# Soft-capped attention and two MLPs on one Trainium2 core: batches 2 and 3 begin twelve slots later

## The chip, the cores and the metric

The kernel runs on one core of a Trainium2 chip. Its engines are TensorE (PE, with its weight loads shown as PEld), VectorE (DVE), ScalarE (ACT), GpSimd (POOL) and SyncE (SP), which here only issues DMAs. The metric is the device time of one execution in microseconds. Each engine takes its instructions in the order in which the built program has them.

## The reference

```
attention, per batch b (4) and head h (12), 448 rows of 64:
  s = q k^T / 8 ; s = cap * tanh(s / cap) ; p = softmax(s) ; o = p v
x  = the heads of o side by side: 1792 rows (4 batches of 448) x 768
h  = max(x w_in, 0)                 768 -> 2048
x2 = h * h @ w_out                  2048 -> 768
h2 = x2 w_in2 ; g = h2 * sigmoid(1.702 h2)
out = g @ w_out2                    1792 x 768
```

All inputs are 32- or 64-bit floats: the weights come as 64-bit words and are put together on the chip.

## The kernel before

**Precision.** A float is split into a high part that TensorE multiplies in one pass and a low part (the rest). A product takes three matmuls of 448 columns: high by high, high by low, low by high.

**MLP units.** The work on one batch's 448 rows is a pass. A pass is 68 units (`PER`): per layer 16 of kind "a" (one block of 128 hidden columns, 18 matmuls, L1240, with an evaluation on ACT and DVE and a split into the tile `g`) and 18 of kind "b" (one block of 128 output columns over 5 or 6 hidden blocks, 15 or 18 matmuls, added into `y`). Below, u0 to u67 are the first pass, u68 to u135 the second, and so on. A unit's weights are split two units ahead, ACT writing `wh` (L1220) and DVE `wl` (L1221). In the first pass the 64-bit words are also loaded from the inputs (L1161), turned into floats (ACT `sx` L1196, DVE `y32` L1203) and stored to DRAM (`keep`, L1214); later passes load those (L1172).

**Attention slots.** A pair is two heads of one batch; there are 24, six to a batch. A pair's steps stand in a table of slots (`PLAN`, for batches 0 and 1 `PLAN0`). Loads of q, k are at slot -17; the preparation of `kk` and `qq` (DVE transposes L840, splits L893, L900, L918, L925, and for batches 2 and 3 a DMA on POOL's queue, L906, that copies half of `kk`) at -8 to -3; then four chunks, two slots apart, each of scores on TensorE (`sps`, L955), tanh and exp on ACT (L966, L970), for batches 2 and 3 a split of the exponentials (ACT `phi` L977, DVE `plo` L981), and the product with v on TensorE (`vps`, L1009). Taking the sums (L1056), the division (L1040, L1042) and so on follow up to slot 15 or 19. `sps` has two buffers, so the third chunk's scores wait for the first chunk's tanh.

**How the two meet.** Batch 0's attention stands before the first pass. During pass s (L1349 to L1361) the slots of batch s+1 are spread over the units, `begin` saying at which slot each pair starts: 8 slots to a pair, and 14 later (`LATE`) for batches 1 to 3, which leaves slots between batch 0's last work and batch 1's first. `ready(b)` is the last slot of batch b. Pairs of the batch behind fall into the slots up to `ready(s + 1)` as well, where their own slots lie below it.

**What sets the order.** The building layer lists all instructions in the order in which these loops emit them and then schedules them by its own estimate of readiness, so an instruction can end up units before or behind the place where it was emitted. What an engine meets is that schedule, shown below where the change moves it.

Names: `mps` is a unit's accumulator, `xt` the input of a pass, `x32` an attention output before its split, `vt` and `vs` tiles of v, `e` the exponentials, `vps` the product with v, `o` a transposed block of the result that POOL's queue stores (L1298).

Of the kernel before, what the change touches and what calls it, by code (L numbers as in the profile page):

```python
# [677 lines left out]
def bounded_cap(ctx, tc, q, k, v, cap, w1, w2, w3, w4, out):  # L678
# [46 lines left out]
    XZ = 2  # L725
    PA = 1
    PB = 4
    LATE = 14

    EARLY = (10, 11)  # L730
    LA = (5, 4, 3, 2)
# [60 lines left out]
    pairs = [(b, p) for b in range(B) for p in range(NP)]  # L792
# [314 lines left out]
        PLAN[2 * c + 4].append((add_keys, c))  # L1107
    ORDER = sorted(set(PLAN) | set(PLAN0), reverse=True)

    begin = [8 * n + (LATE if b else 0) for n, (b, p) in enumerate(pairs)]  # L1110
    first_slot = {t: n for n, t in enumerate(begin)}

    last_split = []
# [264 lines left out]
@with_exitstack  # L1378
def softcap_attention_mlp_mlp(ctx, tc, q, k, v, cap, w1, w2, w3, w4, out):

    nc = tc.nc
    pool = ctx.enter_context(tc.tile_pool(name="flag", bufs=1))
    c = pool.tile([1, 2], F32, name="capsize")
    over = pool.tile([1, 1], I32, name="over")
    nc.sync.dma_start(out=c[:, 0:1], in_=cap.rearrange("(o n) -> o n", o=1))
    nc.vector.tensor_scalar(c[:, 1:2], c[:, 0:1], -1.0, None, ALU.mult)
    nc.vector.tensor_tensor(c[:, 0:1], c[:, 0:1], c[:, 1:2], ALU.max)
    nc.vector.tensor_scalar(over, c[:, 0:1], CAP_MAX, None, ALU.is_gt)
    bounded_cap(tc, q, k, v, cap, w1, w2, w3, w4, out)
    flag = nc.values_load(over, min_val=0, max_val=1)  # L1390
    with tc.If(flag > 0):
        any_cap(tc, q, k, v, cap, w1, w2, w3, w4, out)
# [30 lines left out]
```

## Time and profile before

| | us |
|---|---|
| median of 3 runs | 1208.37 (1207.05 to 1210.19) |
| the profiled execution, device time | 1208.87 |
| its span, first to last instruction | 1207.1 |
| TensorE matmul busy | 1162.8 (96% of the span) |
| DVE busy | 820.2 (68%) |
| ACT busy | 748.2 (62%) |

In this execution the first product of the first pass starts at 79.4 us, u44 at 291.7, u72 at 437.2, the third pass (u136) at 692.4 and the fourth (u204) at 963.3. Times below count from the span's start. In rows of engine sums each pair is busy time with the number of instructions in brackets, and PEclk is TensorE's mean granted clock, 1.00 being 2.4 GHz.

### The profile page before, as it was taken

Reading aid. Unit: us, or ns where it says so; the run is one execution under the profiler, and the core shown is the slowest. Engines: PE = TensorE matmul, PEld = TensorE weight load, DVE = VectorE, ACT = ScalarE, POOL = GpSimd, SP = SyncE. Lnnn points to the kernel's source line nnn. Section 1 sums busy time; section 2 is a strip of 40 time slices with the busy share of each in tenths; the row PEclk is TensorE's granted clock in tenths of the full one; section 3 lists DMA queues with packets and bytes.
Section 4 is the critical chain, followed back from the end, with each engine's and each line's share of the span. In section 5 each row is a group of like instructions: output and inputs, shape, how many; then the busy total and the mean of one; then the engine's idle time right before and its main releaser. Section 6 shows DMA issues by size and latency. Waiting matters only on the chain.

```text
span 1207.1 us, 15331 instructions
## 1 busy us (share of the span) xinstructions
PE 1162.8 (96%) x5532; PEld 1005.7 (83%) x5532; DVE 820.2 (68%) x1135; ACT 748.2 (62%) x1105; POOL 70.0 (6%) x157
## 2 busy tenths in 40 slices
PE   7889999989889999999999999999999999999996
PEld 4459778768767889998898899989999999999995
DVE  3577376765778995789688885888665753565454
ACT  6889676766777774576776666677653444344431
POOL 1000000000000220000000320000000220000000
PEclk9999999989899999999999999999999999999999
DMA  4469778677867965535443643333222442333333
GB/s 110 109 195 295 222 224 254 213 227 214 251 196 223 281 181 136 147 92 140 114 123 103 159 131 104 94 107 105 89 82 97 143 134 92 116 107 110 106 99 49
DMA packets 196583, 180.32 MB, mean 149 GB/s; under 512 B 118290, under 2 KB 167442, under 8 KB 196498
## 3 DMA queue, kind: packets, MB, share of 16 engines
q1 hardware_dynamic: 186706, 168.14, 46.5%
q0 software_dynamic: 4224, 10.43, 3.8%
q10 hardware_dynamic: 5568, 0.69, 0.4%
q8 instruction: 46, 0.75, 0.3%
q14 instruction: 39, 0.32, 0.1%
HBM read 142.25 MB, written 30.67 MB: 143 GB/s over the span
## 4 chain that ended last, share of the span: by engine, by line
PE 92%; ACT 5%; DVE 1%; issue 1%; DMA 0%; SPq 0%; DVEq 0%; ACTq 0%
PE mps L1240 79%; PE vps L1009 7%; PE sps L955 5%; ACT e L970 1%; ACT e L966 1%; PE sums L1056 1%; ACT ct L1024 1%; ACT phi L977 0%; ACT wh L1220 0%; ACT qq L918 0%; ACT kk L893 0%; PE qps L844 0%; PE kps L844 0%; ACT sx L1196 0%; DMA qt<-in_q_dram 0%
## 5 line engine op out<-in xcount | busy, mean ns | idle before, releaser
L1240 PE MATMUL mps<-g,wh 128*128 128x448 f32 x1536 | 442.6, 369 | 4.8 <-ACT wh L1220 4.8
L1240 PE MATMUL mps<-xt,wh 128*128 128x448 f32 x1536 | 441.5, 369 | 4.4 <-DVE x L1026 2.7
L1220 ACT ACTIVATE wh<-wraw 128x768 fp32r<-128x768 f32 (+1 forms) x204 | 164.7, 808 | 261.8 <-PE mps L1240 248.1
L1240 PEld LDWEIGHTS mps<-g,wh 128*128 128x128 f32 x1536 | 289.0, 189 | 36.9 <-ACT wh L1220 5.9
L1240 PEld LDWEIGHTS mps<-xt,wh 128*128 128x128 f32 x1536 | 289.6, 189 | 34.4 <-DVE x L1026 3.4
L1240 PE MATMUL mps<-xt,wl 128*128 128x448 f32 x768 | 284.7, 371 | 0.0
L1240 PE MATMUL mps<-g,wl 128*128 128x448 f32 x768 | 282.9, 369 | 1.0 <-DVE wl L1221 1.0
L1221 DVE TENSOR_TENSOR wl<-wraw,wh 128x768 fp32r<-128x768 f32 (+1 forms) x204 | 185.2, 908 | 135.9 <-ACT wh L1220 132.9
L1240 PEld LDWEIGHTS mps<-g,wl 128*128 128x128 f32 x768 | 145.1, 189 | 14.9 <-DVE wl L1221 1.6
L1240 PEld LDWEIGHTS mps<-xt,wl 128*128 128x128 f32 x768 | 145.2, 189 | 14.7 <-issue 1.0
L1269 ACT ACTIVATE g<-r 128x448 fp32r<-128x448 f32 x128 | 73.6, 575 | 68.7 <-DVE r L1261 34.9
L955 PE MATMUL sps<-qq,kk 64*128 64x448 f32 (+1 forms) x444 | 101.9, 417 | 9.0 <-ACT e L966 4.4
L1270 DVE TENSOR_TENSOR g<-r,g 128x448 fp32r<-128x448 f32 x128 | 79.5, 621 | 45.1 <-ACT g L1269 44.6
L1282 DVE SCALAR_TENSOR_TENSOR y<-mps,y 128x448 f32<-128x448 f32 x96 | 59.6, 621 | 57.1 <-PE mps L1240 56.6
L955 PEld LDWEIGHTS sps<-qq,kk 64*128 64x128 f32 (+1 forms) x444 | 64.0, 194 | 38.4 <-issue 20.7
L966 ACT ACTIVATE e<-sps 128x896 f32<-128x896 f32 x96 | 78.3, 818 | 25.6 <-PE sps L955 19.1
L970 ACT ACTIVATE e<-e,ecap 128x896 f32<-128x896 f32 x96 | 90.7, 946 | 1.9
L1221 DVE TENSOR_TENSOR wl<-y,wh 128x768 fp32r<-128x768 f32 (+1 forms) x68 | 61.6, 906 | 35.2 <-ACT wh L1220 34.3
L1009 PE MATMUL vps<-e,vt 128*128 128x448 f32 (+1 forms) x192 | 76.2, 559 | 5.8 <-ACT e L970 5.2
L1196 ACT ACTIVATE sx<-wraw 128x768 f16<-128x768 bf16 (+1 forms) x68 | 69.5, 1022 | 0.2
L1220 ACT ACTIVATE wh<-y 128x768 fp32r<-128x768 f32 (+1 forms) x68 | 54.5, 802 | 22.5 <-DVE y L1203 21.8
L1203 DVE SCALAR_TENSOR_TENSOR y<-wraw,sx 128x768 int32<-128x768 int32 (+1 forms) x68 | 61.2, 900 | 4.2 <-ACT sx L1196 3.5
(77 smaller groups left out, 921.8 us busy)
## 6 DMA issues: line engine op xcount, KB each, us to landing
wraw<-keep SPq DMA_DIRECT2D x66, 768.0 KB, 4.4
wraw<-in_moe_w_in_dram SPq DMA_DIRECT2D x32, 766.5 KB, 6.3
wraw<-keep SPq DMA_DIRECT2D x36, 640.0 KB, 4.4
keep<-y SPq DMA_DIRECT2D x44, 384.0 KB, 3.5
wraw<-in_moe_w_out_dram SPq DMA_DIRECT2D x24, 638.8 KB, 5.4
wraw<-in_moe_w_out_dram SPq DMA_DIRECT2D x12, 766.5 KB, 6.5
keep<-y SPq DMA_DIRECT2D x24, 320.0 KB, 2.7
kk<-kk POOLq DMA_DIRECT2D x24, 256.0 KB, 3.2
```

Of the source, the lines that this page charges most:

```text
L955: nc.tensor.matmul(ps[:, u, :S], x, y, start=all(t[0] != u for t in todo[:n]), stop=all(t[0] != u for t in todo[n + 1 :]),)
L966: nc.scalar.activation(e, sc.pop((b, p, c))[:, width(c), :S], AF.Tanh)
L970: nc.scalar.activation(e, e, AF.Exp, scale=ecap)
L1009: nc.tensor.matmul(pvp[b, p][j][:, :S], x.rearrange("p a d -> p (a d)"), t, start=c == 0 and all(i[0] != j for i in todo[:n]), stop=c == T ...
L1196: pin(nc.scalar.activation(z, words(n, BF16)[:, :, :, 2], AF.Copy))
L1203: pin(nc.vector.scalar_tensor_tensor(y[:, :kn].bitcast(I32), words(n, I32)[:, :, :, 0], 13, sx[n % XZ][:, :kn], ALU.logical_shift_right, A ...
L1220: pin(nc.scalar.activation(hi[:, :kn], t[:, :kn], AF.Copy))
L1221: pin(nc.vector.tensor_tensor(lo[:, :kn], t[:, :kn], f32(hi[:, :kn]), ALU.subtract))
L1240: nc.tensor.matmul(ps[:, :S], a[:, kk, :], r, start=(kk == 0 and i == 0), stop=(kk == kn - 1 and i == 2),)
L1269: nc.scalar.activation(g[:, 0, :], r, AF.Copy)
L1270: nc.vector.tensor_tensor(g[:, 1, :], r, f32(g[:, 0, :]), ALU.subtract)
L1282: nc.vector.scalar_tensor_tensor(y, ps[:, :S], scale, y, ALU.mult, ALU.add)
```

## The change

One table entry becomes four: batch 1 keeps its 14 slots, batches 2 and 3 get 26.

```diff
-    LATE = 14
+    LATE = (0, 14, 26, 26)
...
-    begin = [8 * n + (LATE if b else 0) for n, (b, p) in enumerate(pairs)]
+    begin = [8 * n + LATE[b] for n, (b, p) in enumerate(pairs)]
```

The first pass still takes slots 53 to 117 (65 of them). Batch 2's first pair begins at slot 122 instead of 110. The second pass takes slots 118 to 181 (64) instead of 118 to 169 (52), the third 182 to 229 instead of 170 to 217 (48 both times). Up to u43 TensorE's order is the same in both programs, and from u132 on attention stands at the same units again.

TensorE at the end of u44 in the program of before (`g`, `wh`, `wl` belong to MLP units; the `sps` x15 are the last three chunks of batch 1's last pair, the x4 batch 2's first):

```order
L1240 MATMUL mps<-g,wl 128x448
L1009 MATMUL vps<-e,vt 128x448 x7
L955 MATMUL sps<-qq,kk 128x448 x15
L1240 MATMUL mps<-g,wh 128x448 x2
L955 MATMUL sps<-qq,kk 128x448 x4
L1240 MATMUL mps<-g,wl 128x448
```

Two more such clusters stand at u52 and u60, and a smaller one at u69. In the changed program the same chunks of batch 1 are spread from u44 to u58, one `vps` pair every second unit and one chunk's `sps` between them; here from the end of u51 to the end of u52:

```order
L955 MATMUL sps<-qq,kk 128x448 x6
L1240 MATMUL mps<-g,wh 128x448 x2
L1240 MATMUL mps<-g,wl 128x448
L1240 MATMUL mps<-g,wh 128x448 x2
L1240 MATMUL mps<-g,wl 128x448
L1240 MATMUL mps<-g,wh 128x448 x2
L1240 MATMUL mps<-g,wl 128x448
L1240 MATMUL mps<-g,wh 128x448 x2
L1240 MATMUL mps<-g,wl 128x448
L1240 MATMUL mps<-g,wh 128x448 x2
L1240 MATMUL mps<-g,wl 128x448
L1009 MATMUL vps<-e,vt 128x448 x2
```

The clusters at u44, u52 and u60 are gone there. A new one stands at the end of u64, still in the first pass: all four chunks of batch 2's first pair, and behind it `vps` of its first chunks up to u66. TensorE in the changed program, from u64's last matmuls into u65:

```order
L1240 MATMUL mps<-g,wl 128x448
L955 MATMUL sps<-qq,kk 128x448 x16
L1009 MATMUL vps<-phi,vs 128x448 x2
L1009 MATMUL vps<-plo,vs 128x448 x2
L1009 MATMUL vps<-phi,vs 128x448 x2
L1240 MATMUL mps<-g,wh 128x448 x2
L1009 MATMUL vps<-plo,vs 128x448 x2
L1240 MATMUL mps<-g,wl 128x448
```

ACT in the changed program over the same cluster (`xt` belongs to the next pass, `kk` and `qq` to batch 2's second pair, `wh<-y_3249` is u65's weights):

```order
L1067 ACTIVATE xt<-x_3133 128x448
L966 ACTIVATE e<-sps 128x896 x2
L970 ACTIVATE e<-e,ecap 128x896
L893 ACTIVATE kk<-kps 64x512 x2
L977 ACTIVATE phi<-e 128x896
L970 ACTIVATE e<-e,ecap 128x896
L966 ACTIVATE e<-sps 128x896
L977 ACTIVATE phi<-e 128x896
L918 ACTIVATE qq<-qps,qs 64x448
L1220 ACTIVATE wh<-y_3249 128x640
```

The weights of u65 come behind the cluster's tanh and exp. On POOL's queue the copies of `kk` for batch 2's second pair, which stood ahead of the first pass's 24 result stores, stand among them:

```order
 L859 MEMSET vt 64x64
-L906 DMA kk<-kk 64x1024 x6
-L1298 DMA out_dram<-o 32x14x32 x24
-L906 DMA kk<-kk 64x1024 x12
+L906 DMA kk<-kk 64x1024 x2
+L1298 DMA out_dram<-o 32x14x32 x12
+L906 DMA kk<-kk 64x1024
+L1298 DMA out_dram<-o 32x14x32 x12
+L906 DMA kk<-kk 64x1024 x15
```

The first copy of that pair now has twelve stores ahead of it, the second all 24. The first two matmuls of its scores stand in u67, the next in u80. From u85 to u131 a pair takes 8 units instead of about 9.7.

## Rows read from the trace of the kernel before

**Rows 1.** The page: busy time of each engine, then tenths in 40 slices.

```profile
PE 1162.8 (96%) x5532; PEld 1005.7 (83%) x5532; DVE 820.2 (68%) x1135; ACT 748.2 (62%) x1105; POOL 70.0 (6%) x157
...
PE   7889999989889999999999999999999999999996
...
PEclk9999999989899999999999999999999999999999
```

**Rows 2.** Engine sums by stage: u44 to u71, u72 to u135, pass four, and 71 us.

```profile
core 0: us, PE busy (x) PEld busy (x) DVE busy (x) ACT busy (x) POOL busy (x), PEclk, DMA share, GB/s
...
291.67:437.20 145.53, 133.30 (x599) 110.26 (x598) 117.12 (x164) 110.07 (x158) 19.38 (x32) 0.96 0.77 229
437.20:692.40 255.20, 255.20 (x1254) 232.23 (x1252) 202.20 (x286) 164.40 (x252) 13.07 (x23) 1.00 0.49 129
...
963.30:1207.07 243.77, 234.10 (x1153) 215.78 (x1151) 120.64 (x170) 94.21 (x148) 7.54 (x12) 0.99 0.34 103
489.00:560.00 71.00, 71.00 (x352) 64.59 (x351) 59.73 (x86) 49.45 (x74) 2.05 (x4) 1.00 0.50 130
```

**Rows 3.** The same sums over the four clusters of attention at u36, u44, u52, u60.

```profile
250.40:263.95 13.55, 8.94 (x41) 4.89 (x39) 10.72 (x16) 11.86 (x17) 0.76 (x4) 0.87 0.61 200
295.40:310.15 14.75, 9.40 (x37) 5.82 (x36) 9.81 (x14) 13.24 (x18) 1.19 (x2) 0.82 0.54 167
341.10:356.20 15.10, 11.67 (x38) 7.31 (x37) 12.15 (x18) 13.27 (x18) 1.01 (x2) 0.89 0.48 151
382.30:396.15 13.85, 11.05 (x46) 7.03 (x45) 12.82 (x17) 13.40 (x20) 1.02 (x2) 1.00 0.64 198
```

**Rows 4.** TensorE's timeline over the cluster at u44: start, us, operation, idle before.

```profile
295.39 4.87 PE L1009 MATMUL vps<-e,vt 128*128 128x448 f32 x14
299.75 1.74 PE L955 MATMUL sps<-qq,kk 64*128 64x448 f32 x12
303.58 0.87 PE L955 MATMUL sps<-qq,kk 128*128 128x448 f32 x3 [2.09 <-ACT e L966]
307.71 1.11 PE L1240 MATMUL mps<-g,wh 128*128 128x448 f32 x2 [3.26 <-ACT wh L1220]
```

**Rows 5.** The chain of waits: its longest unbroken stretch of TensorE.

```profile
924.38 266.68 PE mps L1240 x1314
```

**Rows 6.** Groups by shape, whole run: ACT's operations, busy us, mean ns.

```profile
L970 ACT ACTIVATE e<-e,ecap 128x896 f32<-128x896 f32 x72 | 74.9, 1040 | 1.5
L966 ACT ACTIVATE e<-sps 128x896 f32<-128x896 f32 x72 | 65.6, 912 | 24.1 <-PE sps L955 17.7 <-DVE acc L995 3.2 <-PE vps L1009 3.0
L977 ACT ACTIVATE phi<-e 128x896 fp32r<-128x896 f32 x36 | 34.0, 947 | 0.6
L1220 ACT ACTIVATE wh<-y 128x640 fp32r<-128x640 f32 x24 | 17.5, 728 | 7.9 <-DVE y L1203 7.9
L918 ACT ACTIVATE qq<-qps,qs 64x448 fp32r<-64x448 f32 x24 | 15.9, 663 | 0.4
L893 ACT ACTIVATE kk<-kps 64x512 fp32r<-64x512 f32 x24 | 15.0, 624 | 0.3
```

**Rows 7.** POOL's DMAs, `kk` and `out_dram`: ns min/median/max, and us to landing of `kk`.

```profile
L906 POOL DMA_DIRECT2D kk<-kk x24: 512/512/667, 300.6 to 807.1; - x24
...
DMA to landing us min/median/max: 2.8/3.2/5.2
...
L1298 POOL DMA_DIRECT2D out_dram<-o x72: 634/634/677, 406.9 to 978.8; - x72
```

**Rows 8.** Groups by shape of TensorE from u72 to u135: scores and sums.

```profile
L955 PE MATMUL sps<-qq,kk 128*128 128x448 f32 x76 | 18.8, 366 | 0.0
...
L1056 PE MATMUL sums<-plo,one 128*128 128x448 f32 x8 | 2.9, 368 | 0.0
L1056 PE MATMUL sums<-phi,one 128*128 128x448 f32 x8 | 2.9, 366 | 0.0
```

## The prediction

> **What bounds the kernel now.** I read the page first: TensorE is busy 96% of the span, and in the 40 slices its gaps stand at the start and up to slice 12, that is in attention of batch 0 and in the first pass; behind that it reads 9 to the end [rows 1]. So TensorE sets the time, and only the first pass has anything to give back. Next the sums by stage. From u72 to u135 TensorE is busy 255.20 of 255.20 us at a clock of 1.00, though DVE is busy 202.20 of them. From u44 to u71 it is busy 133.30 of 145.53 us at a mean clock of 0.96 [rows 2]. Then the clusters: in that stretch the attention of batch 1's end and batch 2's start stands in three lumps of about 14 us, and each has TensorE waiting: 5.35 us idle in the one at u44, 3.43 at u52, 2.80 at u60, with clocks of 0.82, 0.89 and 1.00 [rows 3]. The timeline shows why: twelve `sps` go at once, then the third chunk waits 2.09 us for a tanh, and the next unit's first matmul waits 3.26 us for `wh`, because ACT takes tanh and exp of the cluster first [rows 4]. The program order decides that, as each engine takes its own list in order.
>
> **What goes.** The change removes no work: the same matmuls and the same activations stand elsewhere. What it can save is TensorE's waiting. From u44 to u71 that is 145.53 - 133.30 = 12.23 us idle, and what the clock took: a mean of 0.96 between the levels 1 and 0.5 means 8% of 145.53, 11.6 us, at 1.2 GHz, in which half the work is done, 5.8 us lost. Together 18.0 us. The three clusters account for most of it: 11.6 us of idle, and 0.18 x 14.75 + 0.11 x 15.10 = 4.3 us of clock [rows 2, 3]. A little more hides in busy time: a matmul record lasts some 0.37 us [rows 8] while they follow each other at 266.68 / 1314 = 0.203 us [rows 5], so each stop of TensorE counts about 0.16 us of draining as busy. With a dozen stops fewer that is 2 us. I put what goes at 20 us. The three clusters are not in the changed order: batch 1's last chunks drip in between u44 and u58.
>
> **What comes instead, first the cluster at u64.** Batch 2's first pair still runs in the first pass, all four chunks at one point. Its price is worked out from ACT's new order. TensorE does the first chunk's four `sps` (0.8 us); from there ACT has two tanh, an exp, two `kk`, a `phi`, an exp, a tanh, a `phi`, one `qq` and then u65's `wh`: 2 x 0.912 + 1.040 + 2 x 0.624 + 0.947 + 1.040 + 0.912 + 0.947 + 0.663 + 0.728 = 9.35 us [rows 6]. So u65 starts some 10.2 us behind u64's end. Meanwhile TensorE has 16 `sps` and 6 `vps`, 22 x 0.203 = 4.5 us. It loses 5.7 us. The clock may fall behind that as it did in three of the four clusters; their clock losses are 0.13 x 13.55 = 1.8, 2.7, 1.7 and 0 us [rows 3], on average 1.5. Sum 7.2 us. The bounds by the nearest rows are the mildest and the worst cluster, idle and clock together: 2.8 us at u60 and 5.35 + 2.7 = 8.0 at u44. I take 7.2, as ACT's list is the sharper measure; DVE's transposes ahead of `kk` and `qq` hang on loads that SP issues in u62 to u64, and if these land late ACT stands and the price rises, which is why I stay near the upper bound.
>
> **Second, the drip from u44 to u58.** TensorE's share of it is work that it did before as well. New is that no slack is left on the others where layer 2's hidden units end: from u50 to u52 I count ACT's and DVE's lists at about TensorE's own length. Weights stand three to four units ahead there (the `wl` of u56 is made in u53, before in u55), so a lag of a unit is covered; what isn't covered is the eviction of `mps` by DVE. Nearest rows: 0 from u72 to u135, where attention drips in the same way and TensorE never waits [rows 2], and 3.4 us, the idle of one cluster, if it stalls there once. I take 1 us.
>
> **Third, the second pass.** The attention matmuls behind u71 grow by 26 `sps`, 18 `vps` and 8 sums, 52 x 0.203 = 10.6 us. This is moved, not added, so it cancels between the stretches. But the rest gets denser there: DVE's work per unit without attention is 120.64 / 68 = 1.77 us (pass four); from u72 to u135, 202.20 - 64 x 1.77 = 88.7 us belong to attention, over 76 / 16 = 4.75 pairs, 18.7 us a pair [rows 2, 8]. With a pair in 8 units DVE has 8 x 1.77 + 18.7 = 32.9 us; TensorE has 34.4 us (8 units of 16.9 matmuls, 1152 in 68 units, and a pair of 34, at 0.203). DVE comes to 96%; by the same sum it had 89% at 9.85 units a pair, where the densest stretch read shows 59.73 of 71.00, 84%, without a wait [rows 2]. Weights are two units ahead, so short stretches over 100% are covered. I take 1 us; bounds 0 and the 15 us of the DVE rival.
>
> POOL's queue: the first `kk` copy of batch 2's second pair now stands behind twelve stores. The last four of them come from a transpose some 7.6 us behind u64's end, take 4 x 0.634 us, and the copy lands 0.5 + 3.2 us (at most 5.2) later: about 13.9, at most 16 us [rows 7]. The `sps` in u67 that reads it is reached behind 40 matmuls more, at 10.2 + 40 x 0.203 = 18.3 us. The cover is 2 us at the least; cost nothing. Were each store held up by one instruction of DVE's (117.12 us over 164, 0.71 us [rows 2]), the copy would land 8.6 us later and TensorE would wait 4 to 6 us. The Trainium skill, page "SBUF — State Buffer", section "SBUF: two separate sides", and the part after it, speaks for such a hold-up: GpSimd can't write a DMA's descriptors while VectorE holds the port pair they share, and it gives some 620 ns for a DMA alone and 3100 ns beside a copy; by that, an estimate, twelve stores would take 30 us longer and the time would come out near 1220. The trace disagrees: all 72 stores took 634 to 677 ns, beside a DVE that is busy most of the time [rows 2, 7].
>
> **Sum.** -20 + 7.2 + 1 + 1 = -10.8 us; I round the saving to 10, since the drained time is the softest part. It is made against the profiled execution, 1208.87 us, which is 0.5 us over the median of the runs, so the median becomes about 1198.5 us.
>
> **The rivals.**
> Half of it: the drip doesn't hold on the chip. The built order expects tanh and exp a unit or two ahead of each `vps`; where ACT and DVE lag (u50 to u56), TensorE stalls in several places at 1 to 2 us each and the cluster at u64 costs its 8.0. For it: ACT and DVE have no slack from u50 to u52. Against: the weights' lead, and the drip of u72 to u135 that costs nothing. Saving 20 - 8 - 6 - 1 = 5 us, 1203.5 us.
>
> It doesn't do what it says: batch 2's first pair still stands in the first pass, and its cluster, with loads and POOL's copy behind it, could cost what three did. For it: it holds four chunks at once, where those of before held at most three or four in parts. Against: ACT's list is 9.35 us long and TensorE's work in it 4.5; to lose 18 us the cluster would have to last 22 us. 1207 us, no change to speak of.
>
> Slower: DVE becomes the bound in the second pass. If it can't be kept above the share x of the time, a pair and 8 units take 32.9 / x instead of 34.4 us, over six pairs. At x = 0.91 the six lose 10.5 us and eat the gain; that is where it decides. At 0.89, 2.6 us each, 15 us: 1214 us. For it: no long stretch read has DVE over 84%, and DVE takes its list in order, so `wl` stands behind attention work. Against: at 84% TensorE has not waited at all, and the cluster at u60 has DVE at 12.82 of 13.85, 93% [rows 2, 3].
>
> Late stores: POOL's queue held up as worked out above, TensorE waits 5 us in u67, 1203.5 us. For it: the new order on POOL. Against: 634 to 677 ns for every store [rows 7].
>
> **How the numbers follow.** The forecast with its neighbourhood (1193 to 1202 us) has 0.61, half of it 0.20, no change 0.08, DVE as the bound 0.08, late stores 0.03. A measurement can tell about 0.3%, 3.6 us, from no change: faster means under 1204.7, slower over 1212. Faster takes the first whole, 0.16 of half of it and 0.02 of the stores, 0.79; same 0.04 of half of it, 0.07 of no change, 0.01 of DVE and 0.01 of the stores, 0.13; slower the rest of DVE and of no change, 0.08. The range has 1191 below (all 20 go, the cluster costs 2.8, the rest nothing) and 1207 above (the second case whole, and the edge of the third).
>
> **What would show it.** Right: from u44 to u71 TensorE's idle falls from 12.2 to 5 us or less, nearly all of it in one gap group near the end of u64, behind tanh and `wh`; one dip of the clock there instead of two; u72 starts near 415 us, 22 earlier (10.6 of them moved work); and u72 to u135 stays without idle, about 11 us longer. Wrong: idle spread over u50 to u58 behind DVE's `y` or ACT's exp (half of it); a gap at u67 behind POOL's copy; or waits of `mps` for DVE's `wl` between u85 and u131 with DVE over 90% (slower). A time over 1205 us makes the prediction wrong, as does a saving that comes from another stretch than u44 to u71.

## The result, and the profile after

In the runs of one comparison the changed kernel took 1197.88 us (median of 4 runs, 1196.82 to 1200.59) and the kernel before 1207.80 (4 runs). The ratio is 0.9917, with a 95% interval from 0.9897 to 0.9936, so the change saves about 10 us. The profiled execution of the changed kernel took 1200.59 us.

The page of the changed kernel, with the busy time of each engine and the 40 slices:

```profile
span 1198.7 us, 15319 instructions
...
PE 1159.9 (97%) x5532; PEld 1001.3 (84%) x5532; DVE 818.9 (68%) x1135; ACT 747.7 (62%) x1105; POOL 69.9 (6%) x157
...
PE   7889999989998999999999999999999999999996
...
PEclk9999999989999999999999999999999999999999
```

The counts are those of before [rows 1]: no work was added or taken away. Each slice is some 30 us. Before, TensorE read 8 behind the start in slices 9, 11 and 12, the clock in 9 and 11. The ninth, ahead of u44, stays as it was; in the place of the eleventh and twelfth one is left, the thirteenth, and the clock reads 9 in it.

The engine sums of the changed kernel by stage, with the columns of [rows 2]: u44 to u71 as a whole, then its parts u44 to u63, u64 to the start of u67, and from there to u71; then u72 to u135, the third pass, and the fourth:

```profile
289.90:414.20 124.30, 119.21 (x546) 100.24 (x546) 96.90 (x137) 85.70 (x123) 17.32 (x28) 0.99 0.85 252
...
289.90:372.90 83.00, 82.81 (x382) 69.16 (x382) 61.58 (x86) 60.34 (x88) 1.19 (x2) 1.00 0.88 269
372.90:397.00 24.10, 19.21 (x81) 15.14 (x81) 21.90 (x34) 17.05 (x24) 10.59 (x17) 0.93 0.73 213
397.00:414.20 17.20, 17.20 (x86) 15.95 (x85) 13.42 (x20) 8.30 (x13) 5.54 (x9) 1.00 0.89 225
...
414.20:680.70 266.50, 266.18 (x1306) 241.27 (x1305) 220.69 (x312) 188.73 (x286) 14.50 (x26) 1.00 0.49 128
680.70:951.00 270.30, 270.30 (x1329) 246.43 (x1328) 196.55 (x275) 161.37 (x246) 18.39 (x31) 1.00 0.35 106
951.00:1198.73 247.73, 238.46 (x1153) 215.65 (x1151) 120.63 (x170) 94.10 (x148) 7.52 (x12) 0.99 0.33 101
```

Set against [rows 2]: u44 to u71 took 145.53 us and takes 124.30, 21.2 less. Of these 10.6 are the 52 matmuls that moved on (at 0.203 us), and 10.6 are saved. Pass two took 255.20 and takes 266.50, 11.3 more: the moved matmuls and 0.7 us. TensorE's idle time in u44 to u71 fell from 12.23 to 5.09 us, and 4.89 of it lie in the part from u64 on, around the one cluster that is left, where the clock is 0.93 too. From u44 to u63, where three clusters stood [rows 3], TensorE now waits 0.19 us in all.

TensorE's timeline over that cluster (start, us, operation, idle before it and what ended it):

```profile
375.96 1.78 PE L955 MATMUL sps<-qq,kk 128*128 128x448 f32 x8
377.94 1.89 PE L955 MATMUL sps<-qq,kk 128*128 128x448 f32 x8 [0.20 <-ACT e L966]
381.82 0.67 PE L1009 MATMUL vps<-phi,vs 128*128 128x448 f32 x2 [1.99 <-ACT phi L977]
382.94 0.68 PE L1009 MATMUL vps<-plo,vs 128*128 128x448 f32 x2 [0.46 <-DVE plo L981]
384.39 0.67 PE L1009 MATMUL vps<-phi,vs 128*128 128x448 f32 x2 [0.77 <-ACT phi L977]
385.58 1.11 PE L1240 MATMUL mps<-g,wh 128*128 128x448 f32 x2 [0.52 <-ACT wh L1220]
```

All four chunks of batch 2's first pair go at once; then TensorE follows ACT's list, `phi` by `phi` (and once a `plo` of DVE), until `wh` lets u65 begin at 385.58 us, 9.6 us after the cluster's first matmul. It is the pattern of [rows 4], once instead of three times.

The profiled execution alone would give another saving, 1207.07 - 1198.73 = 8.3 us of span. Two differences in it don't belong to the change: u44 starts 1.8 us earlier (a fall of the clock near 220 us that this execution does not have: from 215 to 228 us the mean is 0.87 before and 1.00 here), and the last pass takes 4.0 us longer, for which see the end. Without these two the span is 10.5 us shorter, as the medians say.

### The profile page after: what moved, and what is told of

Same layout as the page of the kernel before. It is cut to its first block, busy times and chain, and to the rows that moved or that the text cites. A ratio compares the mean times of both kernels' runs of the same rounds, so it can differ in the third digit from the quotient of the medians.

```text
span 1198.7 us, 15319 instructions
## 1 busy us (share of the span) xinstructions
PE 1159.9 (97%) x5532; PEld 1001.3 (84%) x5532; DVE 818.9 (68%) x1135; ACT 747.7 (62%) x1105; POOL 69.9 (6%) x157
## 4 chain that ended last, share of the span: by engine, by line
PE 93%; ACT 4%; DVE 2%; issue 1%; DMA 0%; SPq 0%; DVEq 0%; ACTq 0%
PE mps L1240 78%; PE vps L1009 8%; PE sps L955 5%; ACT e L970 1%; PE sums L1056 1%; ACT e L966 1%; ACT ct L1024 0%; DVE y L1203 0%; ACT wh L1220 0%; ACT sx L1196 0%; PE kps L844 0%; DMA qt<-in_q_dram 0%; PE qps L844 0%; DVE wl L1221 0%; ACT phi L977 0%
## 5 line engine op out<-in xcount | busy, mean ns | idle before, releaser
L955 PE MATMUL sps<-qq,kk 64*128 64x448 f32 (+1 forms) x444 | 98.6, 408 | 5.5 <-ACT qq L920 2.3
```

The lines of the kernel that those rows point to most:

```text
L955: nc.tensor.matmul(ps[:, u, :S], x, y, start=all(t[0] != u for t in todo[:n]), stop=all(t[0] != u for t in todo[n + 1 :]),)
```

## The experiments

Their question was whether clusters on TensorE are what costs the time, or merely the amount of attention in the first pass, and where a denser second pass would begin to cost. The kernel before has medians of 1207.2 to 1208.7 us in the comparisons.

**Batch 3 alone later.**

```diff
-    LATE = (0, 14, 26, 26)
+    LATE = (0, 14, 14, 26)
```

> Batch 3 alone begins 12 slots later, (0, 14, 14, 26). Cluster theory (the gain is TensorE's waiting in lumps of attention that the scheduler makes in the first pass where the next pair's q and k are prepared): the three lumps at u44, u52 and u60 are as before, so no gain, 1207 to 1209 us. Load theory (the gain is attention work taken out of the first pass, where ACT and DVE also unpack weights, in proportion to the matmuls taken out): none is taken out, no gain either. A theory in which the later passes gain: 1204 us or less.

Measured: 1205.78 us, ratio 0.9985 (0.9968 to 1.0001), no change that can be told, though the median lies 1.2 us under what both theories gave. The stretch u44 to u71 is that of before:

```profile
290.70:435.90 145.20, 132.98 (x599) 110.27 (x598) 117.39 (x166) 110.03 (x158) 19.35 (x32) 0.96 0.79 233
```

So batch 3's entry alone gives nothing that can be told; the effect comes with batch 2's. Batch 2's without batch 3's was not run.

**Half the delay.**

```diff
-    LATE = (0, 14, 26, 26)
+    LATE = (0, 14, 20, 20)
```

> Batches 2 and 3 begin 6 slots later instead of 12, (0, 14, 20, 20). Of attention's matmuls 92 stand from u44 to u71, against 114 before and 62 changed, but in three lumps again, at u50, u58 and u66 (24, 24 and 26 at once). Cluster theory: three lumps cost about what three did, 1205 to 1208 us. Load theory: 22 of 52 moved, 42% of the 10 us, 1203.5 us.

Measured: 1209.81 us, ratio 1.0008 (0.9994 to 1.0022): no gain, though 22 of the 52 matmuls had moved behind u71. The load theory's 42% of the gain would be a ratio of some 0.9965, outside the interval; the median itself lies above both ranges. The sums of u44 to u71 and TensorE's three largest waits there (engine and line that waits, what for: us in all, times, longest):

```profile
290.60:431.70 141.10, 128.71 (x576) 107.71 (x575) 112.42 (x159) 100.52 (x143) 18.35 (x30) 0.95 0.80 229
```

```profile
PE sps L955 <- ACT e L966: 3.8, 3, 2.4
PE mps L1240 <- ACT wh L1220: 3.1, 1, 3.1
PE vps L1009 <- ACT phi L977: 2.9, 2, 1.8
```

The idle time is 12.4 us, as before, since three clusters remain, at u50, u58 and u66. With less attention in the stretch and as many clusters, TensorE waits as long as before.

**Eight slots more than the change.**

```diff
-    LATE = (0, 14, 26, 26)
+    LATE = (0, 14, 34, 34)
```

> Batches 2 and 3 begin 20 slots later, (0, 14, 34, 34): no lump from u44 to u71, a pair in 7.1 units in the second pass. Cluster theory: the lump at u64 goes too, 5 to 7 us less than the changed kernel, 1191 to 1193 us. Rival, DVE as the bound of the second pass: by the sums per pair and unit DVE comes to 7.1 x 1.77 + 18.7 = 31.3 us of 31.3, so from u85 to u131 TensorE waits for wl or y and what the lump gives is lost, 1198 us or more.

Measured: 1189.93 us, ratio 0.9841 (0.9818 to 0.9864), faster than both kernels and a little under the cluster theory's range. Batch 2's first pair has left the first pass, and with it the cluster at u64. The sums of u44 to u71, u72 to u135, and the dense part of pass two:

```profile
291.30:402.20 110.90, 109.61 (x515) 93.44 (x514) 84.83 (x122) 72.50 (x106) 13.62 (x22) 1.00 0.85 265
402.20:676.50 274.30, 273.83 (x1337) 247.14 (x1336) 232.53 (x327) 202.13 (x302) 18.34 (x33) 1.00 0.50 129
450.20:664.30 214.10, 213.63 (x1046) 192.23 (x1044) 193.41 (x274) 167.81 (x252) 8.48 (x17) 1.00 0.47 121
```

From the changed kernel to this one u44 to u71 shrinks by 13.4 us, of which 31 matmuls x 0.203 = 6.3 are moved and 7.1 are saved: that is what the cluster at u64 had cost. The second pass grows by 7.8 us, 1.5 more than the moved work. Most of that is pace and not waiting: u72 to u83 take 0.207 us a matmul here (232 begin in 47.95 us) and 0.203 in the changed kernel (224 begin in 45.48 us), which the end of this document comes back to.

```profile
402.21:450.16 47.95, 47.95 (x234) 43.54 (x232) 27.25 (x37) 28.12 (x43) 3.60 (x7) 1.00 0.60 154
```

**The kernel before, with TensorE's order alone changed.** `LATE` is 14 again, and TensorE takes the matmuls of u44 to u67 in the order in which the program writes them, which spreads batch 2's over the units.

```diff
+    def hold(ins):
+        return tc.keep_in_program_order(ins) if held[0] else ins
...
-            nc.tensor.matmul(
+            hold(nc.tensor.matmul(
...
+                held[0] = 44 <= n < 68
```

> The kernel before with its 14 slots, but TensorE's instructions emitted from u44 to u67 keep the order of emission: batch 2's first pair stays in the first pass, and no lump of over 8 attention matmuls stands from u44 to u71. Cluster theory: most of the waiting goes though no work is moved between the passes, 1192 to 1198 us. Load theory: nothing is moved, 1205 us or more, with TensorE's waits spread over the same units.

Measured: 1201.21 us, ratio 0.9939 (0.9915 to 0.9963), 7.5 us less, but not as much as I expected. The run does not separate the two theories as it was meant to, for work does move. The schedule of before had pulled matmuls of batch 2 forward, ahead of where the program writes them, and in program order they fall behind u71. The sums of u44 to u71 and of u72 to u135:

```profile
287.54:420.10 132.56, 124.14 (x567) 104.31 (x566) 103.09 (x145) 92.03 (x133) 18.32 (x30) 0.96 0.85 255
420.10:684.79 264.69, 264.56 (x1301) 240.15 (x1300) 216.41 (x304) 183.94 (x278) 14.04 (x25) 1.00 0.46 124
```

From u72 to u135 stand 1301 matmuls, 47 more than before [rows 2]; the change has 52 more. By the load theory that is some 9 of the 10 us, and the clusters are broken up too, so the time does not tell the theories apart. What the run does show is that with no cluster left on TensorE 8.42 us of idle remain from u44 to u71, more than with the change. By TensorE's largest waits and the chain (lines are 5 higher in this kernel):

```profile
PE mps L1245 <- ACT wh L1225: 7.5, 2, 5.6
```

```profile
369.73 0.57 DVE kps L845
370.30 0.62 DVE acc L1000
...
371.19 0.61 DVE g L1275
371.80 1.00 DVE plo L986
372.80 0.53 DVE r L1270
373.33 0.88 DVE y L1208
374.23 0.85 ACT wh L1225
...
375.13 1.82 PE mps L1245 x3
```

The longest wait ends at 375 us: `wh` stands behind the join `y32` (here `y L1208`), and that behind batch 2's work in DVE's list. With TensorE's order mended, the other engines' lists are the next limit; that these are the cause is read from the chain, in which a load of weights of 10.3 us stands further up, and was not tried by itself.

**The whole first pass in program order, on top of twenty slots.** `LATE = (0, 14, 34, 34)`, with the same `hold` for u2 to u67, which also spreads the lumps of batch 1 at u20, u28 and u36.

```diff
-    LATE = (0, 14, 26, 26)
+    LATE = (0, 14, 34, 34)
...
+                held[0] = 2 <= n < 68
```

> LATE = (0, 14, 34, 34), and TensorE's matmuls of u2 to u67 held in the order in which the program writes them, so that batch 1's attention matmuls, which stand in lumps at u20, u28 and u36 (20, 29 and 30 of them), are spread over u8 to u56 at 2 to 6 per unit. Cluster theory: each lump cost 5 to 8 us of TensorE's waiting and clock, as those of u44 to u71 did in the kernel before; most of it goes, and the kernel takes 1173 to 1183 us, with the first pass (u0 to u67) 8 to 15 us shorter than with twenty slots alone. Rival (ScalarE's and VectorE's own lists stay as they are, so that the join and the weights' split come late and the mps matmuls wait for wh instead, as was seen with the kernel before pinned): 1184 to 1191 us, waits of mps for ScalarE's wh in the place of those for e and qq.

Measured: 1197.27 us, ratio 0.9909 (0.9876 to 0.9942), no better than the change and worse than twenty slots alone. Both expectations failed, the first by the most. The amount of attention in each pass is that of twenty slots: from u0 to u71 both have 222 such matmuls, and only their places within the pass differ. TensorE's three largest waits from u0 to u43 (the 2.7 us end as u0 begins and stand with twenty slots alone too), and the sums of u0 to u43 and u44 to u71:

```profile
PE mps L1245 <- ACT wh L1225: 7.1, 3, 3.3
PE mps L1245 <- DVE x L1031: 2.7, 1, 2.7
PE mps L1245 <- DVE wl L1226: 1.0, 4, 0.3
```

```profile
79.30:287.90 208.60, 199.76 (x916) 163.11 (x916) 143.65 (x190) 153.13 (x222) 3.01 (x16) 0.98 0.83 257
287.90:407.10 119.20, 114.71 (x533) 96.74 (x532) 89.89 (x131) 74.91 (x111) 16.07 (x26) 0.99 0.82 244
```

With twenty slots alone u0 to u43 has 6.83 us idle; here it has 8.84. Spreading the lumps on TensorE turned its waits of `sps` for `e` and `qq` into waits for `wh`, and in u44 to u71 it added 3 us of idle (4.49 against 1.29). So "each cluster costs 5 to 8 us" does not hold as a rule: that much came back where batch 2's part of a cluster left the stretch and the order of all engines changed with it, and nothing where the same work was only spread on TensorE.

**Still later.**

```diff
-    LATE = (0, 14, 26, 26)
+    LATE = (0, 14, 40, 40)
```

> LATE = (0, 14, 40, 40): batches 2 and 3 begin 26 slots later than in the kernel before. VectorE theory: about 6.5 units for a pair, 6.5 x 1.77 + 18.7 = 30.2 us of VectorE's work in some 29.4 us of TensorE's, 103%: 1 us lost in each of about 7 pairs, 1196 to 1198 us. Cluster theory: 1187 to 1192 us, as with twenty slots.

Measured: 1190.82 us, ratio 0.9867 (0.9843 to 0.9891).

```diff
-    LATE = (0, 14, 26, 26)
+    LATE = (0, 14, 46, 46)
```

> LATE = (0, 14, 46, 46): batches 2 and 3 begin 32 slots later than in the kernel before, their first attention matmul stands in u86 or later, and their pairs are spread over fewer units of the second pass. Theory that VectorE bounds a second pass that is dense enough (the prediction's slower rival): at about 6.1 units for a pair VectorE has 6.1 x 1.77 + 18.7 = 29.5 us of work in TensorE's 27.9 us, 106%, so TensorE waits some 1.6 us in each of about 7 pairs: about 1200 us, 10 us over the kernel with twenty slots later. Theory that TensorE alone bounds that pass and only clusters cost: 1187 to 1192 us, as with twenty slots (1190), and no wait of TensorE in the second pass above 1 us.

Measured: 1189.82 us, ratio 0.9865 (0.9836 to 0.9895). Both are as fast as twenty slots within their intervals, as the cluster theory had it. A long dense stretch, u88 to u127 with 32 slots:

```profile
457.80:640.60 182.80, 182.66 (x902) 165.88 (x901) 168.17 (x234) 150.98 (x222) 6.12 (x12) 1.00 0.46 120
```

DVE is at 168.17 / 182.80 = 92% and TensorE idles 0.14 us. The gain ends with the last cluster of batch 2 in the first pass, and pushing further neither helps nor harms.

**More work for DVE.** As no delay took DVE far beyond 92% over such a stretch, I gave it work that changes nothing else: for units u84 to u127 of the changed kernel the subtraction that makes `wl` is issued twice, in every second unit and then in each.

```diff
             pin(nc.vector.tensor_tensor(lo[:, :kn], t[:, :kn], f32(hi[:, :kn]), ALU.subtract))
+            if 84 <= n < 128 and n % 2 == 0:
+                pin(nc.vector.tensor_tensor(lo[:, :kn], t[:, :kn], f32(hi[:, :kn]), ALU.subtract))
```

> The changed kernel, with VectorE's subtraction that makes wl issued twice over in every second one of the units u84 to u127 (22 instructions of 0.893 us more, 19.6 us, over some 195 us). VectorE's share of the stretch u85 to u131, 89% without it, goes to about 98%. The prediction's slower rival (VectorE's work comes in lumps, so TensorE begins to wait from a share of 0.91): 6 us or more of waiting for VectorE there, 1204 to 1212 us. Rival to it (VectorE's list runs ahead far enough that only its sum counts): under 2 us of waiting, 1196 to 1200 us.

Measured: 1199.22 us, ratio 0.9932 (0.9907 to 0.9958). The sums of the dense part of the second pass in the changed kernel, and, over the same interval, with the doubled subtraction:

```profile
464.20:668.40 204.20, 203.88 (x1000) 183.99 (x998) 181.51 (x258) 153.47 (x231) 6.47 (x13) 1.00 0.45 119
```

```profile
464.20:668.40 204.20, 203.82 (x1001) 184.81 (x1000) 197.01 (x280) 153.16 (x231) 6.11 (x12) 1.00 0.47 120
```

DVE goes from 89% to 96%, and TensorE's idle time from 0.32 to 0.38 us. So the slower rival, by which DVE can't be kept above some 0.91 of the time without TensorE losing, is refuted.

```diff
+            if 84 <= n < 128:
```

> The same in each of the units u84 to u127 (44 instructions more, 39.3 us): VectorE's share of the stretch would be 108% of TensorE's time. Either theory: the stretch grows by at least 8% of 204 us, 16 us, so 1212 to 1220 us by the sum alone; by the rival of the prediction, which lets lumps cost as well, 1220 to 1235 us. If TensorE still does not wait, VectorE's records don't mean what both theories take them for.

Measured: 1204.44 us, ratio 0.9961 (0.9940 to 0.9982). The sums over 464 to 668 us, 668 to 690 and 690 to 960 here, then over the first and the third of these in the changed kernel:

```profile
464.00:668.00 204.00, 202.96 (x988) 181.97 (x988) 201.17 (x281) 148.21 (x225) 5.10 (x10) 1.00 0.44 114
668.00:690.00 22.00, 22.00 (x110) 19.86 (x109) 21.54 (x35) 13.87 (x20) 8.89 (x15) 1.00 0.69 185
690.00:960.00 270.00, 270.00 (x1324) 245.26 (x1323) 200.51 (x282) 160.71 (x245) 19.00 (x32) 1.00 0.36 108
```

```profile
464.00:668.00 204.00, 203.68 (x999) 184.04 (x999) 181.31 (x259) 153.27 (x232) 6.12 (x12) 1.00 0.45 119
...
690.00:960.00 270.00, 270.00 (x1327) 245.97 (x1327) 196.21 (x275) 160.69 (x246) 17.80 (x31) 1.00 0.34 105
```

The 16 us that both theories asked for did not come. DVE is at 98.6%, TensorE idles 1.04 us, and u84 to u135 takes 2.1 us longer than in the changed kernel (223.1 against 221.0 us). DVE does only 19.9 us more in the stretch; part of the rest of its work slips behind u131, where 668 to 690 us is now at 98% and 690 to 960 has 4.3 us more. And the 44 instructions make DVE's busy time over the whole run only 32.8 us longer (851.7 against 818.9), not the 39.3 of the expectation. Between the two kernels lie 6.6 us by the medians and some 5, give or take 3.5, by the ratios; I can place only those 2.1. The profiled execution also has the slow last pass that is told of at the end.

## Why the prediction was right, point by point

The prediction said 1198.5 us and the median is 1197.88. The saving lies where it was put.

- **What goes.** Forecast: TensorE's idle from u44 to u71 falls from 12.2 to 5 us or less, nearly all in one group behind tanh and `wh`, with one fall of the clock. Measured: 5.09 us, a trace over it, 4.89 of them from u64 on, and one stretch below a clock of 1.00. The waits end at other tiles than forecast: 2.8 us of them at `phi` and 0.8 at `wh`, only 0.2 at tanh; all three stand in the list of ACT that the forecast was worked out from. That the clusters are where the time went is shown by where TensorE waits: with three, three, one and no cluster (before, half the delay, the change, twenty slots) it idles 12.2, 12.4, 5.1 and 1.3 us from u44 to u71, while the matmuls there fall step by step, 599, 576, 546 and 515. Half the delay shows that the amount of attention does not count in proportion. What stays open is how much of the gain comes with breaking clusters up and how much with the work that leaves: no run broke them up with the amount in each pass kept and gained, and program order on top of twenty slots, which kept it, lost.
- **The cluster at u64.** Forecast 7.2 us, with u65 starting 10.2 us behind u64. It started 9.6 us behind; for its 22 matmuls 4.5 us were needed, so 5.1 were lost where 5.7 were forecast, and the clock's mean of 0.93 over 24.1 us makes another 1.7 where 1.5 were. Taking the cluster away saved 7.1 us by the stages, less 1.5 that the second pass gave back. By the medians the ratio went from 0.9917 to 0.9841, some 9 us, give or take 3.6 (the two intervals in quadrature).
- **The drip.** Forecast 1 us, with bounds of 0 and 3.4. It cost 0.19 us of idle from u44 to u63, so "half of it" did not occur. That the weights' lead of a few units covered ACT and DVE was argued, and no run tried it.
- **The second pass.** Forecast 1 us, measured 0.7. But the working behind it was off: it put DVE at 96% and it was at 89%. In u85 to u131, 181.51 - 47 x 1.77 = 98.3 us are attention, 16.4 us for each of the six pairs there (24 exponentials, four to a pair), where I had 18.7. I had divided the work of a stretch by the pairs counted from its scores (76 / 16 = 4.75), and a stretch cut across pairs can hold more of their other work than of their scores: from u72 to u135 of the kernel before stand the divisions of five pairs (20 reciprocals, four to a pair) and the preparation of `qq` of six (12 operations, two to a pair). And the rival's limit, a share of 0.91, is wrong: at 0.92 and at 0.96 TensorE loses nothing that shows, and at 0.986 some 2 us. DVE's attention work in a pass is for the next batch, so it may fall behind for a while.

The row for the six pairs, from the groups of ACT in 464.2 to 668.4 us of the changed kernel, and two of DVE in 437.2 to 692.4 us of the kernel before:

```profile
L970 ACT ACTIVATE e<-e,ecap 128x896 f32<-128x896 f32 (+1 forms) x24 | 22.7, 947 | 0.4
```

```profile
L1040 DVE RECIPROCAL ct<-ct 128x112 f32<-128x112 f32 x20 | 16.0, 827 | 0.0
L925 DVE SCALAR_TENSOR_TENSOR qq<-qps,qs,qq 64x448 fp32r<-64x448 f32 x12 | 8.2, 681 | 0.2
```

- **POOL's stores.** Forecast: no cost. All 72 stores took 632 to 672 ns again, and at u67 TensorE waits 0.32 us for `wh` and not for a copy. The hold-up by VectorE that the Trainium skill describes (page "SBUF — State Buffer", section "SBUF: two separate sides") does not show in this trace either. The Trainium skill ties it there to VectorE operations in a two-port mode, such as an fp32 copy within SBUF, and no run here shows whether any of this kernel's are such; so the prediction's "the trace disagrees" said too much, and only the time of the stores is shown:

```profile
L1298 POOL DMA_DIRECT2D out_dram<-o x72: 632/632/672, 374.0 to 966.8; - x72
```

- **The sum.** -20 + 7.2 + 1 + 1 = -10.8 was forecast; the stages give -21.2 + 11.3 = -9.9, and -10.6 in u44 to u71 alone. The gross term of 20 us can't be read directly; by the net and the cluster it is 10.6 + 7.1 = 17.7, so it was some 2 us high, about the draining that I had added as the softest part. That the forecast of 1198.5 us came within 1 us is in part luck: the sum was 0.9 us too large, and rounding it to 10 took most of that off again.

## What to carry to other kernels

Where one engine sets the time, look for lumps of other work in its list whose answers come from slower engines: what the one at u64 cost was about the length of the slower engine's list minus the work left to do beside it, and moving some work away did not help while as many lumps remained. Move a lump to where it can be spread on all engines; spreading the same work on TensorE's list alone gained nothing here, and TensorE then waited for `wh` instead. Check in the trace where the matmuls stand before a run is taken to have moved nothing: a change of order can move them across a pass. A second engine at 96% of a stretch need not cost anything if the work that it falls behind with is due only later.

## What the runs showed of the hardware that was not expected

The same matmuls at the same granted clock of 1.00 follow each other at one of two paces, about 0.203 and 0.207 us, for long stretches at a time. The longest unbroken stretch of TensorE in the chain of waits, which lies at the program's end (start, us, what), is 266.68 us for 1314 matmuls before [rows 5]. In the changed kernel, with the subtraction doubled in every second unit, and with it doubled in each:

```profile
911.82 271.30 PE mps L1240 x1314
```

```profile
912.93 267.25 PE mps L1242 x1314
```

```profile
916.98 271.14 PE mps L1242 x1314
```

The sums of u204 to u271 in the changed kernel and in the kernel before, both at a clock of 1.00, hold the same work:

```profile
951.00:1187.30 236.30, 235.26 (x1139) 213.02 (x1138) 118.09 (x166) 94.10 (x148) 7.52 (x12) 1.00 0.33 104
```

```profile
963.30:1195.20 231.90, 230.86 (x1138) 213.12 (x1137) 118.10 (x166) 94.21 (x148) 7.54 (x12) 1.00 0.34 106
```

So a matmul takes 0.207 us instead of 0.203 from about u200 on, without a wait. It is not the change, since the kernel with the subtraction doubled in every second unit has the change and the usual pace. Nor is it the last pass alone: u72 to u83 with twenty slots, shown among the experiments, ran at 0.207 too. What sets it stays open; it was worth 4 us in the changed kernel's execution, and one profile of each kernel can mislead by that much.
